# Kv of the next batch right behind x of this one: a reordered attention and GeGLU kernel on one core

## The chip, the cores and the metric

The kernel runs on one core of a Trainium2 chip. The metric is device time in microseconds (us). TensorE (PE) does the matmuls, VectorE (DVE) and ScalarE (ACT) read what they leave in PSUM, GpSimd (POOL) works on SBUF alone, and SyncE (SP) issues nearly all transfers. PSUM has eight banks of 128 x 512 float32 words here called mm0 to mm7.

## The reference

Two layers, one behind the other. First an attention that is linear in the sequence (8 batches, 8 heads, 576 rows, 64 columns), then a gated feed-forward block over all 4608 rows (512 to 1536 to 512):

```python
q_s = softmax(q, axis=-1)            # over the 64 columns of a row
k_s = softmax(k, axis=2)             # over the 576 rows
kv  = einsum('bhsd,bhse->bhde', k_s, v)
x   = einsum('bhsd,bhde->bhse', q_s, kv)     # as 4608 x 512
out = (gelu(x @ w_gate) * (x @ w_val)) @ w_out
```

## The kernel before, in words

A batch has 576 rows: 512 of them (MAIN) are worked as one block of the feed-forward part, the other 64 (REM) go into a tile `xtr`, and the remainders of all eight batches make a ninth block. The order of blocks is 0 to 6, then the ninth (written 8), then 7. The large products are done with Strassen's scheme in Winograd's form: seven products of quarter matrices (128x256 matmuls) in place of eight, with sums and differences of the operands made by DVE and POOL.

The order of all work is written out by hand-like words, one string per block in the table `PROG`; `play` reads them and issues what each word says. The words that matter here, for block b with n = b + 1:

- `0P1` to `2P7`, `6P1` to `8P7`: the seven products of one column block of gate and value. `0c` is ACT's copy of a partial sum to a second bank (L678), `0s5` a scaled copy to SBUF (L657, L659), `0a2` the addition on DVE (L662), `0u` and `0g2` the gelus (L704, L694), `0m2` and `0U` the products of gate and value that fill `ht` (L696, L706).
- `O1` to `O7`: the seven output products (L623) into banks psA, psB, psC; `y1`, `y2`, `y5` scaled copies of them, `b+`, `c+`, `a+`, `yea` what makes the output tile `yo`; `s01` to `s24` sums of `ht` (L496); `x0` to `x3` differences of x (L528); `w61d` and the like sums and differences of the weights (L521).
- `Ek`, `Eq`: ACT's exponentials of k and q of the batch after next (L210); `TE` and `TG` load ACT's tables for exp and gelu (L436). `NA`, `NB`, `M0` to `M3` normalize q; `t` transposes it by DMA. `V0` to `V3` cast v (L220). `lk`, `lv`, `lq` issue the loads.
- `K`: 72 small matmuls (64x64 tiles, L318) for kv of batch n into two banks `pskv`; the denominator comes from a column of ones beside v. `k`: DVE divides by it (L327, L328) and frees the banks.
- `X`: x of batch n (L383): 8 matmuls of 64 columns into two banks `psxr` (the remainder; 16 where two batches share the call) and 8 matmuls of 512 columns into four banks `psx`. `Xa` and `Xd` copy one half of the results each, on ACT and DVE: the remainder first, then the two main banks.

A word behind `<` or `>` belongs to the block before or after. There is one buffer for the exponential of k (`ek`) and one for the cast v (`v16`), so `Ek` of the next batch can be written only when `K` has read the last. Banks come from `ring`: `big` takes the first one, or with `seed` the first that was last filled whole; a bank that is held comes back by `let_go` at the ring's end. Before, each block n from 1 on has `K` for kv of its next batch, then `k`, then `X` of that batch, all near the block's end, with output products between them; `Eq` stands before `Xa` in most blocks and `Ek` behind it, in the next block.

Of the kernel before, what the change touches and what calls it, by code (L numbers as in the profile page):

```python
# [18 lines left out]
def kernel(  # L19
# [74 lines left out]
    def let_go(t):  # L94
        ring.append(held.pop(id(t))[1])

# [213 lines left out]

    def unit_kv4(b, spare=False):

        ps = st[(b, "pskv4")] = [big([P, 2, VW], f32, "pskv", True) if spare else
                                 small([P, 2, VW], f32, "pskv") for _ in range(2)]
        for j in range(2):
            for n in range(NT):
                for a, hh, t, r, o in quarters(j):
                    nc.tensor.matmul(ps[hh][o, j, :], ek_b[0][r, n, a * D:(a + 1) * D],  # L318
                                     v16_b[0][r, n, a, 0:VW], start=(n == 0), stop=(n == NT - 1))
        if not spare:  # L320
            kv4_norm(b)

    def kv4_norm(b):
        kv = st[(b, "kv")] = kv_tile(b)
        for hh, ps in enumerate(st[(b, "pskv4")]):
            rck = att.tile([P, 2], f32, name="rck4", tag="rck4", bufs=2)
            nc.vector.reciprocal(out=rck, in_=ps[:, :, D])  # L327
            nc.vector.tensor_tensor(out=kv[:, hh], in0=ps[:, :, 0:D],  # L328
                                    in1=rck.unsqueeze(-1).to_broadcast((P, 2, D)), op=ALU.mult)
            free(ps)  # L330

# [58 lines left out]
    def free(ps):  # L390
        if id(ps) in held:
            let_go(ps)
# [6 lines left out]

    def unit_x4(b, engs=("act", "dve"), rem=None):  # L400


        psr = [small([P, 4, REM], f32, "psxr") for _ in range(2)]
        for j in range(2):
# [5 lines left out]
        for j in range(2):  # L410
            px.append([big([P, MAIN], f32, "psx", att_ring == []) for _ in range(2)])
            x_mm(b, j, px[j], xq)
        st[(b, "px")] = psr, px, rem
        if engs:
            for t, eng in enumerate(engs):
                x4_out(b, t, eng)

    def x4_out(b, t, eng):
        psr, px, rem = st[(b, "px")]
        copy_on(eng, xtr[:, t:HP:2, b * REM:(b + 1) * REM], psr[t][:, 0:2])  # L420
        if rem is not None:
            copy_on(eng, xtr[:, t:HP:2, rem * REM:(rem + 1) * REM], psr[t][:, 2:4])
        for j in range(2):
            xt_out(b, j, t, eng, px[j][t])
        for p in [psr[t]] + [px[j][t] for j in range(2)]:
            free(p)
# [103 lines left out]
    def product_gv(i, ps, xt, k, first):  # L530
        lo, hi = slice(k * P, (k + 1) * P), slice((k + NO // 2) * P, (k + NO // 2 + 1) * P)
        xs = xs_b[xt is st.get((B - 1, "xt"))]
        for t, w, nm in ((0, wv_sb, "v"), (1, wg_sb, "g")):
# [103 lines left out]
    def play(b, x):  # L637
# [146 lines left out]
        else:  # L784
            {"K": lambda: unit_kv4(n, True), "k": lambda: kv4_norm(n),
             "X": lambda: unit_x4(n, (), 0 if n == B - 1 else None),
             "Xa": lambda: x4_out(n, 0, "act"), "Xd": lambda: x4_out(n, 1, "dve"),
             "t": lambda: unit_td(n), "tr": lambda: unit_trem(0),
# [74 lines left out]
    def cast_o(c):  # L863
# [25 lines left out]
        "E2q": on(exp, "q", 2), "E2k": on(exp, "k", 2), "tr": on(unit_trem, 1), "sh": on(make_s),  # L889
        "K2": on(unit_kv4, 2), "X2": on(unit_x4, 2, (), 1), "one": on(one_ring),  # L890
    }
# [33 lines left out]
```

## Time and profile before

| | |
|---|---|
| runs | 288.12, 289.47, 289.02 us; median 289.02 |
| profiled execution | 288.34 us, span 286.6 us, TensorE clock 0.999 of full speed |
| busy, share of the span | PE 97%, DVE 87%, ACT 74%, POOL 50% |
| matmuls / DVE / ACT / POOL instructions | 2965 / 502 / 392 / 133 |
| HBM read and written | 37.75 and 9.44 MB |
| loads of k, q, v (1152 KB each), median to landing | 9.3, 8.9, 6.8 us |

Times in the profile are from the span's start. A busy PE is a PE with a matmul in flight: ends are modelled and include the pipeline's drain, so what a matmul costs is read from the distance between starts. In a line of the timeline, several like instructions are merged (x12), and the bracket at the end gives the idle time before them and what ended it.

### The profile page before, as it was taken

The page shows a single profiled execution, that of the slowest core. Times are in us where ns is not written, and L with a number is a line of the kernel's source. Part 1 is how long each engine was busy: PE and PEld are TensorE (multiplying, and loading weights), DVE is VectorE, ACT ScalarE, POOL GpSimd, SP SyncE. Part 2 cuts the span into 40 slices and gives each one's busy share as a digit, 9 for nine tenths or more (in the row PEclk, how much of TensorE's full clock was granted, in tenths as well). Part 3 has the DMA queues.
Part 4 walks back from the last instruction along what each step waited for, and adds up shares of the span by engine and source line. Part 5 has one row for each costly group of instructions (what it writes and reads, how often), then busy time and mean ns, then how long its engine had stood idle before and what let it go on. Part 6 is the DMA issues. An engine that isn't in the chain of part 4 may idle for free.

```text
span 286.6 us, 7459 instructions
## 1 busy us (share of the span) xinstructions
PE 279.0 (97%) x2965; PEld 219.5 (77%) x2965; DVE 249.3 (87%) x502; ACT 212.5 (74%) x392; POOL 142.7 (50%) x133
## 2 busy tenths in 40 slices
PE   8999999999899999999999999999999999999994
PEld 3434445478788778888888888888888888888883
DVE  1925898999999998889989998999999799998993
ACT  4763557768997899988998899799794577716840
POOL 1567666995849656765864257542553104110110
PEclk9999999999999999999999999999999999999999
DMA  7999999975559616169149953770306030003303
GB/s 264 394 383 387 409 408 398 319 305 82 168 188 402 143 27 229 75 62 354 50 67 246 361 173 146 218 208 2 146 9 79 0 150 0 2 0 77 73 2 146
DMA packets 39122, 51.26 MB, mean 179 GB/s; under 512 B 16304, under 2 KB 22704, under 8 KB 39088
## 3 DMA queue, kind: packets, MB, share of 16 engines
q1 hardware_dynamic: 38240, 49.13, 53.1%
q10 hardware_dynamic: 848, 1.67, 1.5%
q8 instruction: 23, 0.38, 0.5%
q14 instruction: 11, 0.09, 0.1%
HBM read 37.75 MB, written 9.44 MB: 165 GB/s over the span
## 4 chain that ended last, share of the span: by engine, by line
PE 71%; DVE 2%; issue 1%; ACT 0%
PE psa L540 25%; PE psA L623 14%; PE psc L540 12%; PE psC L623 7%; PE psb L540 6%; PE psB L623 3%; PE pskv L318 2%; DVE cc L662 1%; PE psx L383 1%; PE psxr L383 0%; DVE yo L662 0%; DVE wgv_sb L521 0%; DVE ht L696 0%; DVE yo L806 0%; ACT gl L694 0%
## 5 line engine op out<-in xcount | busy, mean ns | idle before, releaser
L540 PEld LDWEIGHTS <-wgv_sb 128*128 128x128 f16 x720 | 70.3, 98 | 10.1 <-DVE wgv_sb L521 0.9
L540 PE MATMUL psa<-xs,wgv_sb 128*128 128x256 f16 x312 | 43.6, 273 | 0.6 <-DVE wgv_sb L521 0.6
L706 POOL TENSOR_TENSOR ht<-cc 128x512 f16<-128x512 f32 x20 | 25.9, 1295 | 34.4 <-ACT cc L704 31.3
L623 PEld LDWEIGHTS <-ht 128*128 128x128 f16 x384 | 37.1, 98 | 5.3 <-issue 0.4
L235 POOL TENSOR_TENSOR eq<-eq,rrq 128x576 f16<-128x576 f16 (+1 forms) x27 | 31.9, 1195 | 10.4 <-DVE rrq L229 10.0
L704 ACT ACTIVATE cc<-cc 128x512 f32<-128x512 f32 x45 | 28.2, 630 | 7.7 <-DVE cc L662 7.7
L662 DVE SCALAR_TENSOR_TENSOR cc<-psa,snq 128x512 f32<-128x512 f32 x45 | 30.4, 684 | 2.7 <-PE psa L540 1.9
L678 ACT COPY psb<-psa 128x512 f32<-128x512 f32 x45 | 26.0, 585 | 8.9 <-PE psa L540 6.4
L662 DVE SCALAR_TENSOR_TENSOR cc<-psc,snq 128x512 f32<-128x512 f32 x45 | 30.3, 684 | 1.8 <-PE psc L540 1.1
L659 ACT ACTIVATE snq<-psc 128x512 f32<-128x512 f32 x38 | 22.3, 603 | 6.2 <-PE psc L540 5.9
L441 PEld LDWEIGHTS <-wgv_sb 128*128 128x128 f16 x144 | 13.8, 98 | 17.0 <-issue 1.1
L227 DVE TENSOR_REDUCE rq<-eq 128x18 f32<-128x1152 f16 (+1 forms) x16 | 21.1, 1318 | 5.2 <-ACT eq L210 5.2
L623 PE MATMUL psA<-tw,ht 128*128 128x256 f16 x192 | 23.5, 272 | 0.1
L540 PE MATMUL psb<-xt,wgv_sb 128*128 128x256 f16 x156 | 23.4, 272 | 0.0
L540 PE MATMUL psa<-xt,wgv_sb 128*128 128x256 f16 x156 | 22.9, 273 | 0.0
L694 ACT ACTIVATE gl<-psb 128x256 f32<-128x256 f32 x45 | 16.7, 382 | 7.6 <-PE psb L540 7.3
L623 PEld LDWEIGHTS <-sh 128*128 128x128 f16 x192 | 18.5, 98 | 3.1 <-DVE sh L496 0.5
L696 DVE SCALAR_TENSOR_TENSOR ht<-psb,gl 128x256 f16<-128x256 f32 x45 | 18.6, 416 | 2.2 <-ACT gl L694 2.1
L210 ACT ACTIVATE ek<-kt 128x2304 f16<-128x2304 f32 (+1 forms) x10 | 17.3, 1739 | 2.6 <-DMA kt<-in_k_dram 2.5
L696 DVE SCALAR_TENSOR_TENSOR ht<-psa,gl 128x256 f16<-128x256 f32 x45 | 18.4, 415 | 0.9 <-ACT gl L694 0.9
L694 ACT ACTIVATE gl<-psa 128x256 f32<-128x256 f32 x45 | 17.0, 385 | 3.0 <-PE psa L540 2.6
L436 ACT ACT_TABLE_LOAD x13 | 16.7, 1283 | 3.1 <-issue 2.9
(203 smaller groups left out, 659.6 us busy)
## 6 DMA issues: line engine op xcount, KB each, us to landing
qt<-in_q_dram SPq DMA_DIRECT2D x7, 1152.0 KB, 8.9
out_dram<-yo SPq DMA_DIRECT2D x15, 512.0 KB, 3.1
kt<-in_k_dram SPq DMA_DIRECT2D x6, 1152.0 KB, 9.3
vt<-in_v_dram SPq DMA_DIRECT2D x6, 1152.0 KB, 6.8
wgst<-in_moe_w_gate_dram SPq DMA_DIRECT2D x5, 512.0 KB, 7.2
wvst<-in_moe_w_val_dram SPq DMA_DIRECT2D x5, 512.0 KB, 7.3
wost<-in_moe_w_out_dram SPq DMA_DIRECT2D x5, 512.0 KB, 6.4
out_dram<-yo SPq DMA_DIRECT2D x10, 128.0 KB, 2.4
```

What stands on the lines that cost most here:

```text
L210: nc.scalar.activation(out=o.rearrange("p n (a d) -> p a n d", d=D), in_=tiles[(nm, b)][:, 2 * i0:2 * i1, n0 * D:NT * D].rearrange("p a (n ...
L227: nc.vector.reduce_sum(rq, e, axis=mybir.AxisListType.X)
L235: (nc.gpsimd if eng == "pool" else nc.vector).tensor_tensor(out=e, in0=e, in1=rrq.unsqueeze(-1).to_broadcast((P, n, D)), op=ALU.mult)
L540: nc.tensor.matmul(ps[:, t], a, x, start=(first and t == 0 and c == 0), stop=(c == 1), skip_group_check=True)
L623: nc.tensor.matmul(ps[t], a, w, start=(first and j == js[0] and (t == ts[0] or ps[t].tensor is not ps[ts[0]].tensor)), stop=(j == js[-1]), ...
L659: nc.scalar.activation(out=dst, in_=src, func=ACTF.Copy, scale=scale)
L662: nc.vector.scalar_tensor_tensor(out=out, in0=src, scalar=scale, in1=sn, op0=ALU.mult, op1=ALU.add)
L678: nc.scalar.copy(out=t[f"b{k}"], in_=t[f"a{k}"])
L694: nc.scalar.activation(out=gl, in_=t[ps][:, 1], func=ACTF.Gelu)
L696: nc.vector.scalar_tensor_tensor(out=ht[:, k if x[2] == "2" else k + NO // 2, 0:256], in0=t[ps][:, 0], scalar=_H_SCALE, in1=t["g" + ps], o ...
L704: nc.scalar.activation(out=cc[:, :, 1], in_=cc[:, :, 1], func=ACTF.Gelu, scale=1.0 / _H_SCALE)
L706: (nc.vector if side == "dve" else nc.gpsimd).tensor_tensor(out=ht[:, k:k + NO // 2 + 1:NO // 2, 256:512], in0=cc[:, :, 0], in1=cc[:, :, 1 ...
```

## The change

Kv of batch n + 1 is computed directly behind x of batch n (n = 2 to 6), in the columns of the remainder's two banks that x leaves free. `unit_x4` takes the two banks as tiles of 4 x 64 + 2 x 65 words; x's remainder goes to the first 256, kv to the others. The new word `XK` stands for both, `kk` for the normalization that follows (`kv4_norm(n + 1)`), which frees the shared bank. Kv of batch 2 keeps its own call (`K2`), and x of batch 7 has no kv behind it.

`x4_out` copies the main banks first and the remainder last. `let_go` puts a freed bank at the head of the ring if it was not last filled whole, else at its end as before.

The strings of blocks 1 to 6 are new throughout; those of -1, 0, 8 and 7 are as they were. In the new ones `TE` and `Ek` stand before `XK`, `Eq` behind `Xa`, and `lk` behind `Ek`; the order of products differs in places, and a few sums change engine (DVE has 6 instructions fewer, POOL 8 more, ACT one more).

```diff
     def let_go(t):
-        ring.append(held.pop(id(t))[1])
+        tag = held.pop(id(t))[1]
+        ring.insert(len(ring) if tag in full else 0, tag)
...
-    def unit_kv4(b, spare=False):
-
-        ps = st[(b, "pskv4")] = [big([P, 2, VW], f32, "pskv", True) if spare else
-                                 small([P, 2, VW], f32, "pskv") for _ in range(2)]
+    def unit_kv4(b, spare=False, ps=None):
+
+        if ps is None:
+            ps = [big([P, 2, VW], f32, "pskv", True) if spare else
+                  small([P, 2, VW], f32, "pskv") for _ in range(2)]
+        st[(b, "pskv4")] = ps
...
-            free(ps)
+            free(st.pop((b, "psxr", hh), ps))
...
-    def unit_x4(b, engs=("act", "dve"), rem=None):
-
-
-        psr = [small([P, 4, REM], f32, "psxr") for _ in range(2)]
+    def unit_x4(b, engs=("act", "dve"), rem=None, kv=None):
+
+
+        both = None if kv is None else [big([P, 4 * REM + 2 * VW], f32, "psxr", True) for _ in range(2)]
+        psr = ([small([P, 4, REM], f32, "psxr") for _ in range(2)] if both is None else
+               [p[:, 0:4 * REM].rearrange("p (a m) -> p a m", a=4) for p in both])
...
+        if kv is not None:
+            for t in range(2):
+                st[(kv, "psxr", t)] = both[t]
+            unit_kv4(kv, True, [p[:, 4 * REM:4 * REM + 2 * VW].rearrange("p (j e) -> p j e", j=2) for p in both])
...
     def x4_out(b, t, eng):
         psr, px, rem = st[(b, "px")]
+        for j in range(2):
+            xt_out(b, j, t, eng, px[j][t])
         copy_on(eng, xtr[:, t:HP:2, b * REM:(b + 1) * REM], psr[t][:, 0:2])
         if rem is not None:
             copy_on(eng, xtr[:, t:HP:2, rem * REM:(rem + 1) * REM], psr[t][:, 2:4])
-        for j in range(2):
-            xt_out(b, j, t, eng, px[j][t])
...
+             "XK": lambda: unit_x4(n, (), None, n + 1), "kk": lambda: kv4_norm(n + 1),
...
-        "K2": on(unit_kv4, 2), "X2": on(unit_x4, 2, (), 1), "one": on(one_ring),
+        "K2": on(unit_kv4, 2), "X2": on(unit_x4, 2, (), 1, 3), "one": on(one_ring),
```

The end of block 4 and the head of block 5 in the two tables, around x5 (from `O5` or `K` on; block 5's first words follow the bar):

```diff
-K 8a5 8g2 8P4 2g4 2a2 O1:03 8u 2m2 2m4 O1:1 8g4 O1:4 8m2 O1:25 2u 8m4 O2 8U k 2Ud TE s21d X y1a s22d O6 Xa Xd | 0P1 <s24d <x2d <O5 <x0d <s14d <s23d <s13d <Eq 0P5 lq 6P1 0c <b+ 0P2
+O1:25 2u 8g4 TE Ek 8m2 8m4 O2 y1d s12p 8Ud 2U s21d Er b+ O5 XK Xa s14d Xd >0P1 >0c s22p O6 >6P1 >lv kk >lk s13p s24p | <x0d <Eq <x1d lq Rr NB <x3p M2 <x2d 6P5 0P6
```

82 rows, old and new, of the table PROG are left out of this document.

## The prediction

> **What bounds the kernel now.** I read the page first (busy time by engine), then the chain that ended last, the timelines of PE, ACT and DVE at the ends of the batches, and the waits. The page's first row:
>
> ```profile
> PE 279.0 (97%) x2965; PEld 219.5 (77%) x2965; DVE 249.3 (87%) x502; ACT 212.5 (74%) x392; POOL 142.7 (50%) x133
> ```
> ```profile
> PE 71%; DVE 2%; issue 1%; ACT 0%
> ```
> PE is the bound: 97% busy, and 71% of the chain. A change pays only by what it takes out of PE's stream, or puts into it as a wait. PE's timeline shows the joints (columns: start, length, engine, line, operation; in brackets idle time):
>
> ```profile
> 72.46 1.05 PE L623 MATMUL psC<-tw,sh 128*128 128x256 f16 x8 [0.22 <-DVE sh L496]
> 74.03 0.78 PE L318 MATMUL pskv<-v,ek 64*64 64x65 f16 x72 [0.53 <-ACT ek L210]
> ...
> 96.35 0.61 PE L540 MATMUL psa<-xs,wgv_sb 128*128 128x256 f16 x4 [0.59 <-DVE wgv_sb L521]
> ...
> 102.96 1.47 PE L623 MATMUL psC<-tw,sh 128*128 128x256 f16 x12
> 104.37 0.78 PE L318 MATMUL pskv<-v,ek 64*64 64x65 f16 x72
> 105.08 1.48 PE L623 MATMUL psA<-tw,sh 128*128 128x256 f16 x12
> 106.49 0.26 PE L383 MATMUL psxr<-eqt,kv 64*64 64x64 f16 x8
> 106.58 0.61 PE L383 MATMUL psx<-eqt,kv 64*64 64x512 f16 x8
> 107.11 1.16 PE L623 MATMUL psC<-wo_sb,s 128*128 128x256 f16 x9
> ```
> Starts count here, since lengths include the drain. Twelve 128x256 matmuls take 12 x 0.109 = 1.31 us, so the stream before kv is issued at 104.27, yet kv starts at 104.37: about 0.09 us go when PE passes from 128x128 to 64x64 tiles. The same stands before x (105.08 + 1.31 = 106.39, x at 106.49), and behind it (106.58 + two rounds of 0.216 = 107.01, next at 107.11).
>
> ACT at the end of batch 1 (its order is what the change turns round):
>
> ```profile
> 69.82 0.63 ACT L704 ACTIVATE cc<-cc 128x512 f32<-128x512 f32 x1
> 70.47 1.28 ACT L436 ACT_TABLE_LOAD   x1
> 71.76 0.20 ACT L436 ACTIVATE tiny<-tiny 128x1 f32<-128x1 f32 x1
> 71.87 2.11 ACT L210 ACTIVATE ek<-kt 128x2304 f16<-128x2304 f32 x1
> 73.88 2.20 ACT L210 ACTIVATE eq<-qt 128x1152 f16<-128x1152 f32 x2
> 75.99 2.11 ACT L210 ACTIVATE ek<-kt 128x2304 f16<-128x2304 f32 x1
> 78.12 1.28 ACT L436 ACT_TABLE_LOAD   x1
> ```
> From the end of the last gelu (70.45) to the end of exp(k) there are 3.53 us that nothing shortens: table load, the one-column activation, exp. Rows in sequence start some 0.07 us before their forerunner ends, so I count an ACT copy of 0.60 as 0.53, a gelu of 0.38 as 0.30, the 128x512 gelu of 0.63 as 0.56.
>
> **The change, part by part.** The sum is made against the profiled execution: 288.34 us, span 286.6, so 1.74 outside it; it lies 0.68 under the median of 289.02. Half a percent, 1.45 us, is about what a measurement of this kernel can tell from no change.
>
> *Joints.* Kv of batches 3 to 7 (five of them) loses its own pair of joints: 0.09 in, seen above, and out between 0 and 0.13 (the gap behind the last kv matmul in the trace is 0.127, a round of four takes 0.027); I take 0.10, as behind x. 5 x 0.19 = 0.95 us off PE. Bounds 0.45 to 1.1.
>
> *The wait at 96.35.* Product 7P7 waited for DVE's in-place difference of weights (w73), 0.59 idle and 0.75 by starts. In the new order w73 stands directly behind w83, and by row lengths ends some 2 us before 7P7. Minus 0.75 (bounds 0 and 0.75).
>
> *What is moved on ACT.* Exp(k) of batch n+1, which stood behind the copies of x of batch n, now stands before them, for kv follows x at once; exp(q) goes behind them. Table loads stay 14, exps the same; only the order counts. So kv now waits for the chain last gelu, table load, exp(k), and the x copies queue behind exp(k). By boundary, PE's work against ACT's, from the end of the last product before it:
> - x2/kv3. K2 itself keeps its place: behind the last product PE has 3 x 1.31 + 0.09 = 4.02 before it, ACT needs 0.16 + 0.30 + 0.30 + 0.63 + 3.53 = 4.92, so it waits 0.9; before, 0.39 and 0.60 did the same. Then ACT has two exp(q), exp(k) and three casts of v (5.9 us behind the first exp's end) against 5.8 of PE up to the half of kv3 that reads them: 0.1 to 0.2. Behind it the copies of x are earlier than before, since the table load at 78.12 no longer stands ahead of them; two gaps of PE (0.17 at 79.21, 0.20 at 80.88) go. But the table load now falls after 6s5, and the copies 0s5 and those behind it come 0.3 late and at 0.53 each against products of 0.44: 0.5. In all +0.65 against -0.37: +0.3.
> - x3/kv4. PE has 5.15 from the last product (8P4) to kv; ACT 0.16 + 0.30 + 0.56 + 0.53 (y1) + 3.53 = 5.08: no wait. Then ACT owes y5 0.53, two x copies 1.34, the remainder 0.20, y2 0.60 = 2.67 before O7 may overwrite psA, and PE reaches O7 after kv 0.71, a joint 0.10, O3 1.31 = 2.12: wait 0.5.
> - x4/kv5. 5.15 against 0.16 + 0.30 + 0.56 + 3.53 + 0.53 = 5.08; y2 is on DVE here: 0.1.
> - x5/kv6. From the end of the last 2P product PE has 4.93 to kv. ACT has 0.16 + gelu 0.30 + two wide gelus 1.12 + gelu 0.37 + 3.53 = 5.48, since O6 now stands behind kv: wait 0.6 with the semaphore's 0.05. Behind kv comes product 0P1 at once; it wants an x copy that stands behind exp(k) and the exponential of q's remainder: 0.2, and O3 waits 0.15 for y5. Sum 0.95.
> - x6/kv7. DVE's last cc ends 1.45 behind the product, ACT then has 0.56 + 0.30 + a cast 0.58 + y1 0.53 + 3.53 = 5.5; PE 6.68: wait 0.3 to 0.4, and 0.1 at 6P1 for kv's normalization. Sum 0.5.
>
> New waits: 0.3 + 0.5 + 0.1 + 0.95 + 0.5 = 2.35. Bounds: nothing, if ACT runs 0.6 earlier than summed at each; 5 x 0.95 = 4.75, if all are like the worst.
>
> *The shared banks.* The normalization of kv on DVE (0.16 + 0.29 twice, 0.9 us) now follows the remainder's copies and waits for ACT's copy out of the same bank; behind it on DVE stand a+, the x differences and the 1.34 reduction of q. The bank it frees goes to the head of the ring, so 0P1, 6P1 or 0P5 takes it next. By boundary DVE ends it 0.3 us before that product (x3), 1.3 (x4), 0.3 (x5), 0.1 late (x6, counted). Between 0 and 0.9 per boundary; I take the sums.
>
> *Loads.* Loads of k follow exp(k) at once, those of q exp(q); each has some 25 us to its use and lands in 8.9 to 9.3. On SP they stand ahead of stores, which nobody waits for within 5 us, and of the load of v. V of batch 3 waits for POOL's casts, then 6.8 to land, 0.6 us before ACT is free to cast it: 0, up to 4.5 if it took the 11.3 of the slow v loads. DVE has 6 operations less, POOL 8 more (some 9 us of POOL, which was 50% busy): 0 on PE, if POOL doesn't hold up DVE (rival 3).
>
> Sum: -0.95 - 0.75 + 2.35 = +0.65. PE's small gaps within the batches (0.4 us before) I leave as they are. 288.34 + 0.65 = 289.0 for the profiled kind, **289.7** beside the median.
>
> **Rivals.**
> 1. *ACT is never late (faster).* The sums at x5 and x6 hang on 0.6 and 0.4 us of ACT backlog. In the rows of before, some hundred waits of PE end with 0.05 to 1 us to spare, so orders of this kind can fit that closely. Then only joints and w73 count: -1.7, so 287.3. It decides where exp(k) ends before the last x matmul. Against it: ACT's operations from x2 to x3 sum to 25.9 us in the new order, PE's to 26.3.
> 2. *ACT's lateness is carried on.* After x2 the copies behind the table load trail PE by 0.5; if batches 3, 5 and 6 do the same, and x4 waits like x5, 1.5 + 0.6 come on top: 291.8. For it: from x to x DVE is at 88 to 96% and ACT, up to x6, at 87 to 90%, so little is caught up.
> 3. *DVE is held up by POOL.* Two rows of one form:
> ```profile
> 93.00 1.43 DVE L521 TENSOR_TENSOR wgv_sb<-wgv_sb 128x512 f16<-128x512 f16 x1
> ...
> 95.88 0.41 DVE L521 TENSOR_TENSOR wgv_sb<-wgv_sb 128x512 f16<-128x512 f16 x1
> ```
> The long one began as POOL's multiplication of eq ran (92.98 to 94.15). POOL now has 8 more; at kv's boundaries it computes s4 and ht differences while DVE has its own ahead of the x copies. Two such delays of 1.0 less the 0.3 us of room each: +1.4, so 291.1. [...]
> 4. *The joint isn't saved*, because kv waits anyway and PE runs empty: 290.6.
>
> **How the numbers follow.** Forecast 0.45 (288.7 to 290.7), rival 1 0.20 (286.8 to 288.3), rival 2 0.25 (290.8 to 293), rival 3 0.07, rival 4 0.03. Below 287.57 lies three quarters of rival 1: 0.15. Above 290.47 lie rivals 2 and 3, most of 4 and a sixth of the forecast: 0.42. Within: 0.43. Range 287.2 to 292.1: it leaves out the lower half of rival 1 and a third of rival 2, a little under 0.2, and holds the bounds of joints and waits except all at their ends.
>
> **What would show it.** Right: in the profile after, x and kv matmuls adjoin without the 0.09; no wait on wgv_sb L521 near 96; PE waits for ACT's ek at x5 and x6 (0.3 to 0.6 each) and K2's wait stays; ACT's y2 ends after O3 at x3. Wrong: no PE wait for ek but K2's (rival 1); waits for snq or psb copies at the start of most batches (rival 2); DVE rows of 1.0 and more at L505 or L537 ahead of the x copies (rival 3). A v load that lands late, or PE gaps inside the batches, would upset the sum from outside.

## The result, and the profile after

The changed kernel takes 290.9 us (median; 289.15 to 293.08) beside 288.73 (288.12 to 289.47) for the kernel before on the same chip: ratio 1.0077, interval 1.0058 to 1.0096. It is slower by 2.2 us. That lies in my range (287.2 to 292.1), but the sum came out at 289.0 for the profiled kind of execution, and the profiled one took 290.56. The page after, busy time by engine and the first line of the chain that ended last:

```profile
PE 279.5 (97%) x2965; PEld 219.8 (76%) x2965; DVE 247.2 (86%) x494; ACT 212.8 (74%) x393; POOL 153.1 (53%) x140
```
```profile
PE 66%; ACT 5%; issue 1%; DVE 1%
```

PE has the same 2965 matmuls; ACT now holds 5% of the chain, where it had 0%. Against the page before, DVE has 8 instructions fewer, POOL 7 more and ACT one more, where the section on the change says 6, 8 and one. To see where the time went I cut both traces at the same work, by starts (the last records end at 286.56 and 288.77):

| stretch | before | after | difference | predicted |
|---|---|---|---|---|
| start to kv of batch 1 | 45.94 | 46.04 | +0.10 | 0 |
| from there to kv of batch 2 (K2) | 28.09 | 29.42 | +1.33 | 0 |
| K2 to x of batch 7 | 150.32 | 150.66 | +0.33 | +0.65 |
| x of batch 7 to the last DVE instruction | 58.63 | 58.63 | 0 | 0 |
| from there to the end | 3.57 | 4.02 | +0.45 | 0 |

Only the third stretch holds what the prediction was about, the five boundaries. The two large differences lie outside it. The table by stretches (length, then busy time and instructions of PE, PEld, DVE, ACT, POOL, the clock, DMA share, GB/s), first before, then after, shows that in the second stretch nothing was added to PE (180 matmuls each); it stood:

```profile
48.00:74.00 26.00, 25.28 (x180) 16.85 (x176) 24.94 (x43) 20.44 (x37) 20.31 (x15) 1.00 0.78 248
```
```profile
48.00:75.40 27.40, 25.33 (x180) 17.05 (x176) 24.73 (x43) 19.93 (x36) 21.42 (x16) 1.00 0.74 235
```

The wait behind it, in the timelines of PE and ACT after:

```profile
58.11 0.60 PE L549 MATMUL psa<-xt,wgv_sb 128*128 128x256 f16 x4
59.90 1.02 PE L450 MATMUL ps11g<-xt,wgv_sb 128*128 128x512 f16 x4 [1.19 <-ACT gl L727]
```
```profile
54.55 0.62 ACT L727 ACTIVATE gl<-ps6g 128x512 f32<-128x512 f32 x1
58.19 0.67 ACT L189 CAST v<-vt 128x576 f16<-128x576 f32 x1 [3.03 <-DMA vt<-in_v_dram]
58.77 0.59 ACT L727 ACTIVATE gl<-ps8g 128x512 f32<-128x512 f32 x1
59.26 0.59 ACT L727 ACTIVATE gl<-ps10g 128x512 f32<-128x512 f32 x1
```

and ACT before:

```profile
54.48 0.62 ACT L718 ACTIVATE gl<-ps6g 128x512 f32<-128x512 f32 x1
54.96 0.63 ACT L718 ACTIVATE gl<-ps10g 128x512 f32<-128x512 f32 x1
57.43 0.67 ACT L188 CAST v<-vt 128x576 f16<-128x576 f32 x1 [1.84 <-DMA vt<-in_v_dram]
58.01 0.59 ACT L718 ACTIVATE gl<-ps8g 128x512 f32<-128x512 f32 x1
```

In both kernels ACT stands still for the last chunk of batch 2's v (the word `@d3:a`), whose load was issued near 49.2 and landed 8.2 us later before, 8.9 after. Before, the gelu of 10g is done by then and only 8g waits behind the cast. In the new string of block 1 the cast stands ahead of both gelus; 11g wants the bank that the gelu of 10g frees, and PE stands still with it, 1.35 by starts. K2's own wait is as long as what it replaces: 1.10 by starts after, 0.39 and 0.69 in two places before.

PE's timeline after, at the places that the prediction shows of before (K2 and x of batch 2; 7P7, here at 98.96; x of batch 3) and at x of batch 5:

```profile
73.05 1.47 PE L632 MATMUL psC<-tw,sh 128*128 128x256 f16 x12
75.46 0.81 PE L321 MATMUL pskv<-v,ek 64*64 64x65 f16 x72 [0.94 <-ACT ek L211]
...
80.38 0.60 PE L386 MATMUL psx<-eqt,kv 64*64 64x512 f16 x8
80.81 0.95 PE L321 MATMUL psxr<-v,ek 64*64 64x65 f16 x72
...
98.53 0.60 PE L549 MATMUL psb<-xt,wgv_sb 128*128 128x256 f16 x4
98.96 0.60 PE L549 MATMUL psa<-xs,wgv_sb 128*128 128x256 f16 x4
...
107.55 0.71 PE L386 MATMUL psx<-eqt,kv 64*64 64x512 f16 x8
107.98 0.91 PE L321 MATMUL psxr<-v,ek 64*64 64x65 f16 x72
108.82 1.48 PE L632 MATMUL psC<-wo_sb,s 128*128 128x256 f16 x12
...
165.10 0.61 PE L386 MATMUL psx<-eqt,kv 64*64 64x512 f16 x8
165.71 0.78 PE L321 MATMUL psxr<-v,ek 64*64 64x65 f16 x72
166.64 0.60 PE L549 MATMUL psa<-xt,wgv_sb 128*128 128x256 f16 x4
```

Kv follows x without 128x128 work between; the wait for w73 is gone; K2 still waits, 0.94. From x's first main matmul to kv's first it is 0.43 at x3, about two rounds of x's 64x512 matmuls (0.219 each by starts), and 0.61 at x5. At x5 kv waits, but little: ACT's exp(k) ends at 165.66, and kv starts at 165.71.

```profile
163.55 2.11 ACT L211 ACTIVATE ek<-kt 128x2304 f16<-128x2304 f32 x1
```

### The profile page after: what moved, and what is told of

Same layout as the page of the kernel before. It is cut to its first block, busy times and chain, and to the rows that moved or that the text cites. A ratio compares the mean times of both kernels' runs of the same rounds, so it can differ in the third digit from the quotient of the medians.

```text
span 288.8 us, 7449 instructions
## 1 busy us (share of the span) xinstructions
PE 279.5 (97%) x2965; PEld 219.8 (76%) x2965; DVE 247.2 (86%) x494; ACT 212.8 (74%) x393; POOL 153.1 (53%) x140
## 4 chain that ended last, share of the span: by engine, by line
PE 66%; ACT 5%; issue 1%; DVE 1%
PE psa L549 23%; PE psA L632 14%; PE psc L549 12%; PE psC L632 7%; PE psb L549 5%; PE psB L632 3%; PE psxr L321 1%; ACT L445 1%; PE psx L386 1%; ACT psb L687 1%; ACT ek L211 1%; ACT gl L703 1%; ACT cc L713 1%; DVE cc L671 0%; PE psxr L386 0%
## 5 line engine op out<-in xcount | busy, mean ns | idle before, releaser
L715 POOL TENSOR_TENSOR ht<-cc 128x512 f16<-128x512 f32 x23 | 29.3, 1277 | 39.4 <-ACT cc L713 37.0
L668 ACT ACTIVATE snq<-psa 128x512 f32<-128x512 f32 x29 | 17.3, 605 | 3.1 <-PE psa L549 3.0
```

What stands on the lines that cost most here:

```text
L668: nc.scalar.activation(out=dst, in_=src, func=ACTF.Copy, scale=scale)
L715: (nc.vector if side == "dve" else nc.gpsimd).tensor_tensor(out=ht[:, k:k + NO // 2 + 1:NO // 2, 256:512], in0=cc[:, :, 0], in1=cc[:, :, 1 ...
```

## The experiments

Medians are of 4 to 12 runs each. The kernel before ran beside each group: 288.73 for E1 to E4, 288.94 for E5 to E8, 288.64 for E9 to E12.

**E1: is it the cast?** Only the word is moved:

```diff
-7v:01 7v:23 8g @d3:a <x1d 7va 8ga 10g lk 10ga 10v
+7v:01 7v:23 8g <x1d 7va 8ga 10g lk 10ga @d3:a 10v
```


> The changed kernel with one word of block 1 moved: ACT's cast of v of batch 2 (@d3:a) stands behind the gelu 10ga, no longer ahead of 8ga and 10ga. Theory A (the largest part of the loss is the 1.35 us by starts that PE loses before 11g, since ACT waits 3.03 us there for the load of v with the gelus that free banks queued behind it): 1.3 us faster than the changed kernel, ratio to the kernel before about 1.003, and less scatter, since the load's landing no longer reaches PE. Rival B (the loss is made at the block ends, and a gap in block 1 is only slack that comes back as waits before K2 or x2): within 0.4 us of the changed kernel, ratio 1.006 or more.

289.27 (289.09 to 290.7), ratio 1.0027 (1.0009 to 1.0044): 1.6 of the 2.2 us come back. Columns as before, ACT and PE of E1:

```profile
55.99 0.60 ACT L727 ACTIVATE gl<-ps10g 128x512 f32<-128x512 f32 x1 [0.45 <-DVE ht L730]
57.73 0.67 ACT L189 CAST v<-vt 128x576 f16<-128x576 f32 x1 [1.14 <-DMA vt<-in_v_dram]
```
```profile
57.99 0.60 PE L549 MATMUL psa<-xt,wgv_sb 128*128 128x256 f16 x4
58.43 1.03 PE L450 MATMUL ps11g<-xt,wgv_sb 128*128 128x512 f16 x4
```

ACT still waits for the load; nobody waits for ACT.

**E2: the same order in the kernel before.**

```diff
-6ga 10ga 6va @d3:a 8ga 9v 8v
+6ga 6va @d3:a 8ga 10ga 9v 8v
```


> The kernel before with the gelu 10ga put behind the cast of v and 8ga, as the changed kernel has it. Theory A: PE waits there for a bank, 0.3 to 1.4 us, and the whole is slower by as much, ratio 1.001 to 1.005. Rival B: no change, ratio 1.000, since block 1 of the kernel before issues 10g earlier and has other banks free.

289.17 (288.24 to 290.0), ratio 1.0006 (0.9986 to 1.0025): no clear loss. In the profiled execution the load happened to land early, 6.7 us after its issue, and the cast began at 55.99. Over ten profiled executions of this case the load took 6.7 to 9.4 us, so the price of a place right behind it differs from run to run. More than that E2 does not settle.

**E3: K2's wait.** On E1, `K2` is put behind the next output product:

```diff
-y5d @K2 s14d s13d Eq O6 lv
+y5d s14d s13d Eq O6 @K2 lv
```


> As e1, and K2 (kv of batch 2) behind O6 in place of ahead of it, so that PE has 1.31 us more work before it needs the exponential of k. If K2's wait (0.94 idle in the changed kernel) hangs only on ACT's chain gelu, table load, exp(k): that wait goes, 0.6 to 1.0 us faster than e1, ratio to the kernel before 0.999 to 1.001. If ACT's second exp(k) and the casts of v, which start only when K2 has read ek, are the next bound: kv3 waits as much longer and it is within 0.3 us of e1.

289.39, ratio 1.0032 (1.0015 to 1.0048): nothing gained on E1. K2 no longer waits; O6 does, for DVE's copy out of the bank, and a second wait for such a copy, 0.34 by starts, follows at 77.69:

```profile
73.87 1.48 PE L632 MATMUL psA<-tw,sh 128*128 128x256 f16 x12 [0.71 <-DVE gl L666]
75.28 0.80 PE L321 MATMUL pskv<-v,ek 64*64 64x65 f16 x72
```

**E4: w73 alone, in the kernel before.**

```diff
-8P1 w83d 1P4 1m2 2a2 7P2 2a5 8c 8P6 7P5 7s2 w73d 7P7
+8P1 w83d w73d 1P4 1m2 2a2 7P2 2a5 8c 8P6 7P5 7s2 7P7
```


> The kernel before with the weight difference w73 directly behind w83, as the changed kernel has it; nothing else. If the 0.75 us by starts that PE loses at 96.35 is only the place of w73: 0.6 to 0.8 us faster, ratio 0.997 to 0.998. If DVE is full there, the operations pushed back by 0.42 to 1.4 us (snq, cc, ht) make PE wait in its place: ratio 0.999 to 1.001.

288.5, ratio 0.9992 (0.9979 to 1.0004). The 0.75 at 7P7 goes, but 0.55 of it comes back two products later:

```profile
96.79 0.60 PE L540 MATMUL psc<-xs,kt 128*128 128x256 f16 x4
97.78 0.61 PE L540 MATMUL psc<-xt,sh 128*128 128x256 f16 x4 [0.39 <-ACT cc L704]
```

The operand `sh` there is the next difference of weights, w74, which DVE writes from 97.31 to 97.72. The bracket names ACT; that it is w74 which PE waits for, E12 shows.

**E5: the rest of E1's spread.** E1's profiled execution has a stall at 130: POOL's cast of batch 5's v waits 3.13 us for its load, its product then runs beside DVE's, and PE ends up waiting for DVE (DVE, POOL and PE of E1):

```profile
126.62 1.65 DVE L715 TENSOR_TENSOR ht<-cc 128x512 f16<-128x512 f32 x1
```
```profile
123.67 1.52 POOL L187 CAST v<-vt 128x576 f16<-128x576 f32 x2 [3.13 <-DMA vt<-in_v_dram]
126.28 1.44 POOL L715 TENSOR_TENSOR ht<-cc 128x512 f16<-128x512 f32 x1
```
```profile
130.68 1.03 PE L549 MATMUL psa<-xs,wgv_sb 128*128 128x256 f16 x8 [0.66 <-DVE cc L671]
```

```diff
-XK Xa s24p y2a s04d            (block 2)
-<c+ <O4 0P6 lv NA              (block 3)
+XK >lv Xa s24p y2a s04d
+<c+ <O4 0P6 NA
```


> E1 with the load of batch 5's v issued ahead of the load of q in place of behind it (before: some 3 us later). Theory: most of E1's runs lie at 289.1 to 289.3 and three of ten a full microsecond above, because POOL's cast waits for that load (3.1 us idle to 123.67 in E1's profile) and the sums behind the cast come late. Then the high runs go and the median is 289.1 to 289.2. Rival: the high runs have another cause; then they stay, at 290 and more in about a third of the runs.

289.21 (289.04 to 289.77), ratio 1.0009 (0.9990 to 1.0028): with these two words moved, the new order can no longer be told from the kernel before. The runs of E1 at 290.03, 290.36 and 290.7 have no counterpart. POOL's cast begins at 121.19 with no wait for the load, and the stall is gone. It need not be the only cause of high runs: E6 and E7, built on E5, have one of ten each above 290. (The profiled execution of E5, 289.69, lost 0.6 before kv of batch 1.)

**E6 and E7: what is a joint worth?** A matmul of one column on the whole array, five times, between x and kv (E6) or ahead of x (E7), on E5, with the shared banks two words wider:

```diff
+            nc.tensor.matmul(both[0][:, 386:387], ident, warm[:, 0:1], start=True, stop=True)
             unit_kv4(kv, True, [...])                                          # E6
+        if both is not None:
+            nc.tensor.matmul(both[0][:, 386:387], ident, warm[:, 0:1], start=True, stop=True)
         for j in range(2):
             x_mm(b, j, [p[:, j] for p in psr], xqr)                            # E7
```


> E5 plus a matmul of one column on the whole 128x128 array between x and kv, five times, so that kv has its own pair of joints again. Compared with E7, which has the same five matmuls ahead of x. My prediction's price of a pair is 0.19 us (0.094 in, 0.10 out): 0.95 above E7, or 0.6 if kv waits for exp(k) at two of the five anyway and the joints hide in that wait. Rival (joint not saved): no difference above 0.2.

> E5 plus the same five matmuls of one column, ahead of x, where PE comes from 128x128 tiles anyway: 5 x 0.02 to 0.06 us, so 0.1 to 0.3 above E5.

E6 289.49, E7 289.19: 0.30 for the five (0.48 between the two profiled executions), less than the 0.95 or 0.6 that I expected. By starts, from x's last matmul to the product behind kv, E6 takes 1.13, 1.16, 1.15, 1.33 and 1.13 at x2 to x6, E7 1.09, 0.97, 0.97, 1.33 and 1.00. So a pair of joints costs 0.19 and 0.18 where little or nothing else is awaited (x3, x4), 0.13 at x6, and 0.04 or nothing at x2 and x5, where kv or the product behind it waits anyway. At x4, E6 and then E7:

```profile
136.17 0.18 PE L422 MATMUL psxr<-warm,ident 128*128 128x1 f16 x1
136.28 0.80 PE L321 MATMUL psxr<-v,ek 64*64 64x65 f16 x72
137.02 1.26 PE L633 MATMUL psC<-wo_sb,s 128*128 128x256 f16 x10
```
```profile
135.46 0.60 PE L386 MATMUL psx<-eqt,kv 64*64 64x512 f16 x8
135.92 0.81 PE L321 MATMUL psxr<-v,ek 64*64 64x65 f16 x72
136.66 1.27 PE L634 MATMUL psC<-wo_sb,s 128*128 128x256 f16 x10
```

**E8: the kernel before with both words moved.**

```diff
-10ga 6va @d3:a 8ga 9v 8v   ...   w83d 1P4 ... 7s2 w73d 7P7
+10ga 6va 8ga @d3:a 9v 8v   ...   w83d w73d 1P4 ... 7s2 7P7
```


> The kernel before with ACT's cast of batch 2's last v chunk behind the gelu 8ga, and w73 directly behind w83 as in E4. If the late landing of that load is what splits the runs of the kernel before into two groups (288.1 to 288.4 and 289.0 to 289.5), only the lower group is left: 288.2 to 288.4. If not, 288.5 as E4.

288.21 (8 of 10 runs from 288.08 to 288.49) beside 288.94; ratio 0.9978 (0.9955 to 1.0001). The runs of the kernel before reach down to 288.05 too, but more than half of them lie above 288.9. So the kernel before seems to pay for the same load in part of its runs; the interval just reaches no change. E4's profiled execution shows one such run, where the load took 9.1 us: a PE wait of 0.58 for the copy behind the late cast and 8ga.

**E9 and E10: the end.** In every profiled execution of the new order but E9's, 4.00 to 4.02 us lie between the start of the last DVE instruction and the end, in every one of the old but E10's 3.56 to 3.57. Of the DMA by queues, after, from 286.9 on:

```profile
DMA packets 15, 0.01 MB, mean 4 GB/s; under 512 B 9, under 2 KB 14, under 8 KB 14
## 3 DMA queue, kind: packets, MB, share of 16 engines
q14 instruction: 1, 0.01, 0.7%
```

A block of 8192 bytes of instructions is on record there, which the old order has not. POOL's drain starts 0.44 after its semaphore clear in place of 0.13, and lasts 0.17 in place of 0.03. I took the one for the cause of the other. POOL has 199 instructions recorded, control instructions included, 190 before. So both kernels get memsets of one column on POOL at the start, 24 on E5 (E9), 9 on E8 (E10):

```diff
+    pad = const.tile([P, 32], f32)
     make_identity(nc, ident)
+    for i in range(24):            # E10: 9
+        nc.gpsimd.memset(pad[:, i:i + 1], 0.0)
```


> E5 plus 24 one-column memsets of POOL at the program's start. In every run of the new order so far 3.98 to 4.01 us lie between the last DVE instruction and the end, in every run of the old one 3.54 to 3.56; the difference lies between POOL's last semaphore clear and its drain, and the trace has a DMA of 8192 bytes of kind instruction there that the old one has not. Theory: POOL's program has become 9 instructions longer, so that its last ones lie in a block that is fetched only then. With 24 more the fetch comes earlier, while POOL is idle anyway: 3.55 us at the end, median 0.44 below E5 (288.7 to 288.8). Rival: the end depends on something else that the new order has; then it stays at 4.0.

> E8 (the old order with two words moved) plus 9 such memsets of POOL at the start, which makes its program as long as the changed kernel's. Theory: the fetch falls at the end, 4.0 us behind the last DVE instruction in place of 3.55, median 288.6 to 288.7. Rival: 3.55 as before.

The end did as said: 3.57 in E9, where no block is fetched there, and 4.01 in E10, where one is. So the 0.44 goes with the number of POOL's instructions, and the late fetch with it. That the drain waits for this fetch is not shown, and the order of the records speaks against it: after, the block's packet starts at 289.06, which is 0.69 behind the start of the drain and 0.29 behind the last recorded instruction.

The times did not do as said: 291.02 and 290.98, because both lose 1.7 us before kv of batch 1 (47.68 and 47.75 in place of 45.9 to 46.1). The loads of the weights run slower there. From 8 to 42 us, E8 and E10, moved bytes and a load of 512 KB to landing:

```profile
DMA packets 9858, 13.46 MB, mean 396 GB/s; under 512 B 461, under 2 KB 6605, under 8 KB 9855
...
wgst<-in_moe_w_gate_dram SPq DMA_DIRECT2D x5, 512.0 KB, 7.1
```
```profile
DMA packets 9406, 12.49 MB, mean 367 GB/s; under 512 B 431, under 2 KB 6575, under 8 KB 9403
...
wgst<-in_moe_w_gate_dram SPq DMA_DIRECT2D x5, 512.0 KB, 8.2
```

E9 and E10 share the memsets and the new tile of 128 bytes per partition, which is declared ahead of nearly all others. Which of the two slows the loads was not tried alone. The traces speak for the tile: 24 memsets cost no more than 9, they end at 1.6 us (E10) and 2.1 (E9), and the loads are slow long after that, at 349 GB/s between 11 and 29 us in E10, 385 in E8.

**E11: how near is ACT to the edge?** One more ACT copy ahead of the table load of exp in blocks 2 to 5, on E5:

```diff
+    def te(b):
+        if 2 <= b <= 5:
+            nc.scalar.copy(out=warm, in_=warm)
+        preload(ACTF.Exp)
```


> E5 plus one more ACT copy of 128x512 (0.5 us) ahead of the table load of exp in blocks 2 to 5, that is in the path to kv of batches 4 to 7 as my prediction summed it. My sums: ACT has 0.07 to spare at x3 and x4 and nothing at x5; so kv there would start 0.4, 0.4 and 0.5 later, x6 0.5 later, some 1.8 in all, 291.0. Rival (ACT is never late, rival 1 of the prediction): there is slack of half a microsecond, and the median stays within 0.4 of E5.

290.9, that is 1.7 above E5 (2.0 if each is measured against the kernel before of its group), against 1.8 said. From the first x matmul to the first of kv it is 0.96, 0.62, 1.19 and 1.10 at x3 to x6, where E5 has 0.52, 0.55, 0.69 and 0.61. Block 3 loses another 0.29 behind kv. The copy adds 0.54 to ACT's sequence. So at x3, x5 and x6 kv starts 0.44 to 0.50 later for it; at x4 there was 0.4 to spare that my sum didn't have. x3 and x5 in E11:

```profile
106.97 0.78 PE L321 MATMUL psxr<-v,ek 64*64 64x65 f16 x72 [0.16 <-ACT ek L211]
...
165.48 0.78 PE L321 MATMUL psxr<-v,ek 64*64 64x65 f16 x72 [0.50 <-ACT ek L211]
```

**E12: w74 early too, in the kernel before.** On E8:

```diff
-1m2 2a2 7P2 2a5 8c 8P6 7P5 7s2 7P7 s01d 8P5 7g2 w74d 1g4
+1m2 2a2 w74d 7P2 2a5 8c 8P6 7P5 7s2 7P7 s01d 8P5 7g2 1g4
```


> E8 with the next difference of the weights, w74, moved from behind 7g2 to behind 2a2, because PE still waits 0.55 at 96.5 for it there. If DVE's place is all that makes it late: 0.3 to 0.5 below E8, 287.8. If the wait moves on to the next product, as it did in E4: within 0.15 of E8's 288.2.

288.28 (288.06 to 289.13), ratio 0.9986 (0.9976 to 0.9996). The 0.55 is gone from its place, and 0.11, 0.23 and 0.23 stand at 98.0, 99.1 and 101.3, where E8 had 0.05 or less: K2 to x of batch 7 is 0.07 shorter than in E8. The wait moved on, as in E4. E8 and E12 are the versions to keep; they are below both kernels, by 0.4 to 0.7 us against the one before, with an interval that excludes no change in E12 and just reaches it in E8.

## Why the prediction was right, and where it was wrong

The range held, and the sum had the right sign. My chances did not choose a side (slower 0.42, within half a percent 0.43); it was slower. The sum did not hold: it was made of the boundaries, and of the 2.2 us they are 0.33. That the time lies in the range is luck as far as its cause goes, for 1.33 and 0.45 of it come from places to which the sum gave nothing. By its steps:

- **Joints, -0.95: right in price.** 0.18 to 0.19 per pair measured where kv waits for little else (E6, E7). In this order only 0.30 of it reaches the end, since at x2, x5 and partly x6 a wait takes what a joint leaves. My 0.027 for a round of four kv matmuls is in no trace: by starts most rounds take 0.029 to 0.036 before.
- **The wait at 96.35, -0.75: right for the new order, wrong as a price of w73.** It is gone after. In the old order the same word brings 0.2 at most (E4), for the next difference of weights was as late. I did not name what would be late next there.
- **New waits, +2.35: too many by about 0.5, and only in part the ones I summed.** By starts, after: x2 +0.43 net of the two gaps that went (0.3 said), x3 0.42 (0.5), x4 0.02 (0.1), x5 0.6 to 0.75 (0.95), x6 0.25 (0.5). Of my kind are the late copies behind x2 (0.22, three of 0.05, 0.27) and 0.21 at 0P1 behind x5, which ACT's copy of x releases. At x3 O7 starts 0.11 late where I had 0.5. Other waits, which I did not have, made up for what was missing: 0.31 at 120.17 for a copy of ACT's, 10 us behind x3; 0.21 at 164.47 for a sum on DVE, ahead of x5; 0.20 at 192.81 for `ht` from DVE, ahead of x6. So the single sums are near in part by luck. Together with the joints and w73 the three terms give +0.0 to +0.2; measured +0.33, the rest in smaller gaps that I did not add up.
- **Kv's wait for exp(k): the term of these that was mis-sized.** From x's last matmul to kv's last it is 0.83 at x3, 0.97 at x5, 0.88 at x6, so the wait is 0.14 and 0.05 at x5 and x6, where I had 0.6 and 0.3 to 0.4. E11 says that the mechanism stands all the same: half a microsecond more on ACT makes kv start nearly that much later at x3, x5 and x6 (0.44 to 0.50). My sums also took ACT's rows to start 0.07 before their forerunner's end; before, it is 0.10 (median of 258, middle half 0.09 to 0.12), so each row in sequence adds some 0.03 less than I summed.
- **"V of batch 3 ... 0, up to 4.5 if it took the 11.3 of the slow v loads": the right kind of risk at the wrong load.** What cost 1.33 was batch 2's v. The step that failed is "PE's small gaps within the batches (0.4 us before) I leave as they are", and with it that the sum begins at x2: block 1's string is new throughout, and I did not go through it for waits on a DMA that change their place on a queue. The row was there before: ACT idle 1.84 for `vt` at 57.43. That row says that everything behind `@d3:a` is late by what the load is late, and the new string puts 10ga behind it. I named a late v load as what would upset the sum from outside; it was inside, in a word that the diff moves.
- **The end, +0.45: not in the sum.** "POOL 8 more ... 0 on PE" was right for PE, and the end still grew with their number (E9, E10); by what mechanism stays open.
- **Rival 1 (ACT never late):** the sign I gave for it came, for PE's list of waits, which leaves out gaps under 0.15, has `ek` at K2 alone. Its mechanism falls all the same: exp(k) ends behind x's last matmul at x4, x5 and x6 (137.44, 165.66 and 196.31 against 137.26, 165.33 and 196.07), and E11 finds 0.1 or less to spare at x3, x5 and x6.
- **Rival 2 (lateness carried on), 291.8,** is nearest to the time and wrong in cause: behind x2 the gaps came as summed (0.22, three of 0.05, 0.27) and behind x3 there is one of 0.31, behind x5 and x6 nothing of the kind.
- **Rival 3 (DVE held up by POOL):** its sign came too. Ahead of x5's copies, DVE and POOL after:

```profile
164.93 1.00 DVE L505 TENSOR_TENSOR s<-ht,sh 128x512 f16<-128x512 f16 x1
```
```profile
164.50 1.16 POOL L505 TENSOR_TENSOR sh<-sh,ht 128x512 f16<-128x512 f16 x1 [1.29 <-DVE sh L505]
```

Two more DVE rows like it, of 1.04 and 1.38, stand at 192.68 and 221.52. No wait of PE can be put down to the first: ACT's copies of x5 start with DVE's (165.87 and 165.86), and ACT's releases 0P1. Before, only 8 of DVE's 71 rows at L496 (mean 0.44) meet a POOL row at all, and the three that lie wholly beside POOL's rows took 0.57, 0.57 and 1.29. A price shows in E1: DVE's product of 1.65 beside POOL's of 1.44, 0.69 for the same row after; it took a late load (POOL's wait of 3.13) to bring the two together. Why a row beside POOL's takes longer, and why 0.57 in one place and 1.29 in another, no run shows.
- **Rival 4 (joint not saved)** holds at x2 and x5 alone.

## What to carry to other kernels

Before costing a rewritten order, list the instructions that wait for a DMA in each engine's string, and see what newly stands behind them; a wait that nobody feels is a price tag for the next one in line. A copy put nearest to its load's median can also turn the load's spread (6.7 to 9.4 us here) into spread of the kernel: 289.15 to 293.08 after, 289.09 to 290.7 in E1, where the cast stands behind the two gelus. When a wait is removed, look a product or two on: three of the waits here (K2's, w73's, w74's) came back behind the next word.

## What the runs showed of the hardware

- Instructions are fetched in blocks while the kernel runs: the trace after has 48 DMA packets of kind instruction, 23 of 16384 bytes and 18 of 8192 among them (23 and 17 before). With 9 more instructions on POOL (E10) a block of 8192 is fetched at the very end, and POOL's last instructions take 0.44 us longer after all work is done: 3.57 against 4.01 us from the last DVE instruction to the end. With 24 more on the new order (E9) both are gone again. That the one causes the other is not shown.
- One tile of 128 bytes per partition and a few memsets at the head of the program slowed the loads between 8 and 42 us from 396 to 367 GB/s (E8, E10), 1.7 us up to kv of batch 1. The cause stays open.
- At x2 and x3 kv directly behind x starts 0.43 us after x's first 64x512 matmul, about two rounds of 0.219, though x's last matmul started only 0.21 (x2) and 0.12 (x3) before. Why it can start so soon behind the last one, no run shows.
